# GpSimd makes part of the elementwise sums, and FFN1 of tiles 6 and 7 goes by seven products, in a fused attention and ELU feed-forward kernel

## The chip, the cores and the metric

The kernel runs on one core of a Trainium2 chip. A core has five engines that run side by side: TensorE (PE in the profile, its weight loads PEld), VectorE (DVE), ScalarE (ACT), GpSimd (POOL) and SyncE (SP). The metric is the device time of one execution in microseconds (us). Lower is better.

## The reference

```python
k_all = concat([beacon_k, k], axis=2)          # B=8, H=8, S=576, D=64, 16 beacon keys
scores = q @ k_all^T / sqrt(64)                # causal on the 576 own keys, beacons always seen
a = exp(scores - max); a /= a.sum(-1)
attn = a @ concat([beacon_v, v], axis=2)
x = attn.transpose(0, 2, 1, 3).reshape(4608, 512)
h = x @ w_in                                   # 512 -> 2048  (FFN1)
g = where(h > 0, h, exp(min(h, 0)) - 1)        # ELU
out = g @ w_out                                # 2048 -> 512  (FFN2)
```

Inputs and output are float32. The kernel computes in 16-bit types with float32 accumulation in PSUM.

## The kernel before

Attention goes batch by batch (b = 0 to 7), the feed-forward part by token tiles: tiles 0 and 1 have 256 tokens each, tiles 2 to 9 have 512. The whole program is one list of short step names, `run("""...""")`, written out as a planner left it. Each engine carries out its own instructions in the order of that list and waits by semaphores for what it needs. `S` makes scores on TensorE, `x` their exponential on ScalarE, `m` masks on VectorE. `D.b.d.n` adds the key chunk n+1 of four heads onto a running sum over chunks (L396), so that TensorE makes the softmax sums (`L`, L422) from one chunk instead of five. `n` and `M` turn sums into scale factors and scale the result into `xT`.

FFN1 of a 512-token tile has 16 steps `F.t.i` (L514), each 4 matmuls of 512 columns into one PSUM bank (tag `hps`, two banks). The ELU of a bank is `e` (exp, ScalarE, L524), `u` (relu, L530 on ScalarE or, as `u.v`, L532 on VectorE) and `k` (min of exp-1 and relu, VectorE, L544), or `e`, `r` (L551) and `g` (L556).

FFN2 of every tile but tile 0 alone (0 and 1 together) is a 2x2 block product by seven products instead of eight (`Q`, L618, 112 matmuls of 256 columns a tile). It needs block sums of the activations, `Z.t.1` to `Z.t.4` (L566, 2048 columns each), and of `w_out`, `wt.1` to `wt.4`, made once. `J` drains its products (L628, L633, L635).

FFN1 of the last two tiles (8 and 9) goes by seven products as well: groups `P.t.g.ph` (L706), four groups of 512 features a tile, each 7 x 4 matmuls of 256 columns in place of four `F` steps. They need sums of `w_in`, `H.n.g` (two instructions of 256 columns each) and of the inputs, `X.t.n` (512 columns, L689). `K` drains them: products 0, 2 and 3 are copied out by ScalarE (L716), and products 1, 4 and 5 are added to such a copy by VectorE (L719), so that `E`, `U` and `V` (L728, L735, L737, L745) can make the ELU.

All elementwise sums (`D`, `Z`, `wt`, `H`, `X`) run on VectorE here. GpSimd issues the input loads (`lq`, `lv`, `lk`, `wi`, `wo`) from its queue and does the beacon copies `lp` (L786). SyncE issues the transposing loads `lt` and the output stores.

Of the kernel before, what the change touches and what calls it, by code (L numbers as in the profile page):

```python
# [8 lines left out]
FP32 = mybir.dt.float32  # L9
# [8 lines left out]
def kernel(  # L18
# [12 lines left out]
    P = 128  # L31
# [163 lines left out]
    def bank(tag, dt=FP32, name="bk"):  # L195
        return psum.tile([P, 512 if dt == FP32 else 1024], dt, tag=tag, name=name)
# [184 lines left out]

    presum = {}
# [5 lines left out]
    @step  # L388
    def D_(b, d, n):

        r_ = presum[b, d] = qkp.bitcast(FP16)[:, :, 0:S]
        t = et4(b, d)
        a, e, col = next((a, e, col) for (j, a, e, col) in lays[b] if j == n + 1)
        rows = kc[n + 1]
        o = r_[0:rows, :, a:e]
        nc.vector.tensor_tensor(  # L396
            out=o, in0=t[0:rows, :, a:e] if n == 0 else o, in1=t[0:rows, :, col:col + e - a], op=ALU.add)
# [120 lines left out]
    def flat(y):  # L518
        return y.rearrange("c n w -> c (n w)")
# [45 lines left out]
    def sub(o_, a_, b_, op_=ALU.subtract, eng="v"):  # L565
        (nc.vector if eng == "v" else nc.gpsimd).tensor_tensor(out=o_, in0=a_, in1=b_, op=op_)  # L566

    HP = NPR // 2

    @step  # L570
    def wt(n, h_):
        c = slice(HP * h_, HP * (h_ + 1))
        if n == 1:
            sub(T1[:, c], B12[:, c], B11[:, c])
        elif n == 2:
            sub(T2[:, c], B22[:, c], T1[:, c])
        elif n == 3:
            sub(B12[:, c], B22[:, c], B12[:, c])
        else:
            sub(T4[:, c], B21[:, c], T2[:, c])  # L580
# [92 lines left out]
    def H_(n, g):  # L673
        for kk_ in range(2):
# [4 lines left out]
            sub(o_, x_, y_, f_)  # L679
# [6 lines left out]
    def X_(t, n, eng="v"):  # L686
# [6 lines left out]
          (0, (1, 0), 3, False), (1, 4, (1, 1), False), (0, (1, 1), 4, False)]  # L693
    hx, fm, hb = {}, {}, {}

    @step
    def P_(t, g, ph):
        if (t, g, 0) not in hx:
            for n_ in (0, 1) if g % 2 == 0 else (1, 0):
                hx[t, g, n_] = bank("hps", name="hps").rearrange("c (n w) -> c n w", n=2)  # L700
        n_, a_, b_, first = PF[ph]
        for c in range(2):
# [9 lines left out]
    def K_(t, g, ph, eng="s"):  # L712
        src = flat(hx[t, g, PF[ph][0]])
# [8 lines left out]
    def hsrc(t, g, ph):  # L722
        return flat(hx[t, g, 0]) if ph == 6 else hb[t, g, ph]
# [76 lines left out]
    wm.4 wm.4 warm.4 wm.4 lq.0.0.0.4 lq.0.1.0.4 wm.4 warm.4 ident lq.0.0.4.8 wm.4 T.0.1.0 bt  # L800
    warm.4 lq.0.1.4.8 bk cb.0.3 T.0.0.0 cb.0.1 cb.0.0 ck.0.1.0 S.0.1.0 ck.0.0.0 T.0.1.1 x.0.1.0
    S.0.0.0 x.0.0.0 T.0.0.1 cq.0.1.1 S.0.1.2 cq.0.0.1 T.0.3.0 S.0.0.2 x.0.1.2 T.0.2.0 x.0.0.2
    cq.0.3.0 S.0.0.3 cb.0.2 lq.1.0.0.4 S.0.3.0 T.0.3.1 cq.0.2.0 x.0.0.3 lv.0.0.1 cq.0.3.1
    x.0.3.0 T.0.2.1 S.0.0.1 tri wm.4 x.0.0.1 S.0.3.2 x.0.3.2 S.0.1.3 cq.0.2.1 x.0.1.3 wm.4 wm.4
    S.0.2.0 wm.4 wm.4 x.0.2.0 S.0.3.3 wm.4 x.0.3.3 S.0.2.3 x.0.2.3 wm.4 m.0.3.0 S.0.3.1 cb.1.0
    x.0.3.1 lv.0.2 m.0.1.0 m.0.2.0 m.0.0.0 L.0.A m.0.1.2 n.0.A m.0.0.2 T.1.0.0 wi.2 m.0.3.2
    cq.1.0.0 S.0.2.1 W.0.A.1 x.0.2.1 W.0.A.0 S.0.1.1 x.0.1.1 T.1.1.0 M.0.A.1 S.0.2.2 M.0.A.0
    x.0.2.2 F.0.5 cq.1.1.0 e.0.5 lv.0.3.4 m.0.2.2 wi.1 m.0.0.3 m.0.1.3 S.1.5 S.1.1 x.1.5 m.0.3.3
    F.0.4 x.1.1 lq.1.0.4.8 wi.0 m.0.2.3 L.0.B cb.1.1 e.0.4 W.0.B.1 n.0.B S.1.3 cb.1.3 u.0.4.v
    M.0.B.1 u.0.5.v F.0.2 x.1.3 e.0.2 r.0.2 S.1.4 x.1.4 S.1.0 x.1.0 F.0.3 T.1.3.0 ck.1.3.0  # L810
    W.0.B.0 g.0.2 wi.3 k.0.4 S.1.12 m.1.0.0 k.0.5 M.0.B.0 e.0.3 F.0.1 x.1.12 T.1.2.0 S.1.10
    r.0.3 g.0.3 F.1.0 cq.1.2.0 cb.1.2 e.0.1 u.0.1 x.1.10 k.0.1 F.1.1 e.1.0 S.1.8 lq.2.0.0.4
    u.1.1.v u.1.0 k.1.0 x.1.8 F.0.0 e.1.1 S.1.9 S.1.6 u.0.0.v lq.2.0.4.8 F.0.6 k.1.1 x.1.9
    lp.3.1 e.0.0 T.2.1.0 F.1.3 x.1.6 u.0.6.v e.0.6 cq.2.1.0 S.1.11 cb.2.0 lv.1.0.1 e.1.3 x.1.11
    S.1.7 k.0.0 F.0.7 S.1.2 u.1.3.v F.1.5 x.1.7 x.1.2 T.2.0.0 k.0.6 lv.1.2.3.4 u.0.7.v e.0.7
    m.1.1.1 T.2.2.0 ck.2.0.0 u.1.5.v ck.2.2.0 m.1.1.0 wo.1 e.1.5 m.1.0.1 F.1.6 wo.3 k.0.7 L.1.1
    L.1.0 wo.0 F.1.2 e.1.6 wo.2 k.1.5 lk.3.0 u.1.6.v lk.3.1 F.1.4 cb.2.1 cb.2.2 n.1.1 M.1.1.0
    W.1.0 k.1.6 n.1.0 M.1.0.0 u.1.2 W.1.1 lv.2.2.3.4 u.1.4 M.1.0.1 lk.4.0 e.1.2 lv.3.2.3.4 k.1.3
    S.2.4 e.1.4 x.2.4 F.1.7 M.1.1.1 k.1.4 u.1.7 e.1.7 F.2.13 T.2.3.0 S.2.8 u.2.13 k.1.7 F.2.12
    e.2.13 x.2.8 F.2.9 u.2.12 cq.2.3.0 S.2.3 e.2.12 k.2.13 S.2.1 e.2.9 wt.1.0 k.1.2 x.2.3 F.2.2  # L820
    e.2.2 lv.2.0.1 Z.1.3.B Q.1.0.7 x.2.1 Q.1.7.14 u.2.9.v S.2.2 S.2.0 u.2.2 k.2.12 F.2.6 k.2.9
    Q.1.14.21 x.2.0 x.2.2 F.2.15 cb.2.3 wt.1.1 e.2.6 wt.2.1 u.2.6 u.2.15 Q.1.21.28 e.2.15
    m.2.0.0 S.2.6 S.2.5 wt.2.0 F.2.4 J.1.0 x.2.5 F.2.10 Z.1.1.B Z.1.2.B S.2.11 x.2.6 Q.1.28.35
# [121 lines left out]
```

## Time and profile before

| | before |
|---|---|
| runs | 330.08, 330.23 (median), 334.53 us |
| profiled execution | 329.86 us, of which the span is 328.2 us, clock 1.000 |
| PE busy | 318.5 us (97%) |
| PEld busy | 215.7 us (66%) |
| DVE busy | 296.9 us (90%) |
| ACT busy | 276.4 us (84%) |
| POOL busy | 85.2 us (26%), nearly all of it issuing DMAs |

Busy time is the time in which at least one instruction ran. An instruction's own duration is somewhat longer than its share of busy time, since neighbours on one engine overlap by some 0.08 us. The span runs from the first to the last instruction; 1.7 us of the execution lie around it.

### The profile page before, as it was taken

The page shows a single profiled execution, that of the slowest core. Times are in us where ns is not written, and L with a number is a line of the kernel's source. Part 1 is how long each engine was busy: PE and PEld are TensorE (multiplying, and loading weights), DVE is VectorE, ACT ScalarE, POOL GpSimd, SP SyncE. Part 2 cuts the span into 40 slices and gives each one's busy share as a digit, 9 for nine tenths or more (in the row PEclk, how much of TensorE's full clock was granted, in tenths as well). Part 3 has the DMA queues.
Part 4 walks back from the last instruction along what each step waited for, and adds up shares of the span by engine and source line. Part 5 has one row for each costly group of instructions (what it writes and reads, how often), then busy time and mean ns, then how long its engine had stood idle before and what let it go on. Part 6 is the DMA issues. An engine that isn't in the chain of part 4 may idle for free.

```text
span 328.2 us, 8827 instructions
## 1 busy us (share of the span) xinstructions
PE 318.5 (97%) x3648; PEld 215.7 (66%) x3648; DVE 296.9 (90%) x527; ACT 276.4 (84%) x449; POOL 85.2 (26%) x109
## 2 busy tenths in 40 slices
PE   7879999999999999999999999999999999999995
PEld 4656766566555655566555665566665888888884
DVE  2677998999998999999989989999999999999992
ACT  2979999998889897999999888988699598889930
POOL 8973791742705626004010500000000000000000
PEclk9999999999999999999999999999999999999999
DMA  9999999999999999995922792010110021111113
GB/s 115 169 190 206 172 167 185 151 151 154 174 173 154 136 172 151 188 116 61 160 82 58 77 106 84 12 34 2 66 34 33 2 96 34 34 65 34 35 64 128
DMA packets 130520, 34.65 MB, mean 106 GB/s; under 512 B 112816, under 2 KB 130480, under 8 KB 130480
## 3 DMA queue, kind: packets, MB, share of 16 engines
q0 software_dynamic: 95840, 18.49, 69.1%
q1 hardware_dynamic: 33920, 15.34, 23.8%
q8 instruction: 28, 0.46, 0.6%
q10 hardware_dynamic: 720, 0.26, 0.3%
q14 instruction: 12, 0.10, 0.1%
HBM read 37.22 MB, written 15.34 MB: 160 GB/s over the span
## 4 chain that ended last, share of the span: by engine, by line
PE 72%; DMA 12%; ACT 7%; POOL 4%; DVE 3%; issue 2%; DVEq 0%; POOLq 0%
PE ops L618 27%; PE hps L514 22%; DMA v<-in_v_dram 10%; PE hps L706 8%; PE sc L318 5%; ACT et L333 5%; PE ut L376 5%; PE sx L618 2%; POOL scr L769 1%; POOL v L149 1%; DMA kst<-in_k_dram 1%; ACT e L524 1%; POOL w_out L163 1%; DVE qkp L396 1%; PE lt L422 1%
## 5 line engine op out<-in xcount | busy, mean ns | idle before, releaser
L333 ACT ACTIVATE et<-sc 128x1024 f16<-128x1024 f32 (+2 forms) x114 | 104.2, 968 | 8.1 <-PE sc L318 7.6
L514 PE MATMUL hps<-xT,w_in 128*128 128x512 f16 (+1 forms) x512 | 110.7, 353 | 0.3 <-DVE gt L556 0.3
L618 PEld LDWEIGHTS <-gt 128*128 128x128 f16 x864 | 83.0, 98 | 21.1 <-issue 2.9
L524 ACT ACTIVATE e<-hps 128x512 f32<-128x512 f32 x112 | 66.7, 615 | 9.0 <-PE hps L514 4.1
L514 PEld LDWEIGHTS <-w_in 128*128 128x128 f16 x512 | 46.8, 98 | 39.0 <-issue 5.5
L544 DVE SCALAR_TENSOR_TENSOR gt<-e,r 128x512 f16<-128x512 f32 x103 | 68.6, 683 | 2.2 <-ACT e L524 0.7
L618 PE MATMUL ops<-w_out,gt 128*128 128x256 f16 x416 | 54.7, 273 | 0.0
L618 PE MATMUL ops<-wt,gt 128*128 128x256 f16 x400 | 53.6, 273 | 0.0
L530 ACT ACTIVATE r<-hps 128x512 f16<-128x512 f32 x74 | 45.0, 616 | 4.5 <-PE hps L514 4.3
L149 POOL DMA_DIRECT2D v<-in_v_dram x40 | 36.4, 1016 | 3.5 <-DMA v<-in_v_dram 1.9
L566 DVE TENSOR_TENSOR gt<-gt 128x2048 f16<-128x2048 f16 (+1 forms) x30 | 33.1, 1110 | 0.1
L338 DVE TENSOR_TENSOR et<-et,triu 128x1024 f16<-128x1024 f16 (+4 forms) x66 | 26.6, 447 | 1.8 <-ACT et L333 1.7
L532 DVE TENSOR_SCALAR r<-hps 128x512 f16<-128x512 f32 x29 | 19.9, 685 | 4.0 <-ACT e L524 3.2
L376 PEld LDWEIGHTS <-v 128*32 128x32 f16 (+1 forms) x800 | 17.2, 96 | 9.4 <-issue 1.2
L745 DVE SCALAR_TENSOR_TENSOR gt<-e,r 128x512 f16<-128x512 f32 x32 | 21.5, 683 | 0.5 <-ACT kst L716 0.4
L376 PE MATMUL ut<-et,v 128*32 128x464 f16 (+3 forms) x560 | 21.1, 296 | 0.3 <-DMA v<-in_v_dram 0.3
L396 DVE TENSOR_TENSOR qkp<-qkp,et 128x1344 f16<-128x1344 f16 (+2 forms) x33 | 19.2, 583 | 0.4
L635 DVE TENSOR_TENSOR osb<-ops,sm 128x512 f32<-128x512 f32 x26 | 17.7, 682 | 1.3 <-PE ops L618 1.3
L716 ACT COPY kst<-hps 128x512 f32<-128x512 f32 x24 | 13.9, 589 | 4.8 <-PE hps L706 4.6
L474 DVE TENSOR_TENSOR xT<-ut,rl 128x672 f16<-128x672 f32 (+12 forms) x26 | 16.4, 669 | 0.7 <-PE ut L376 0.4
L618 PE MATMUL ops<-w_out,s 128*128 128x256 f16 x128 | 16.9, 273 | 0.0
L618 PEld LDWEIGHTS <-s 128*128 128x128 f16 x144 | 13.9, 98 | 2.5
(118 smaller groups left out, 415.7 us busy)
## 6 DMA issues: line engine op xcount, KB each, us to landing
out_dram<-osb SPq DMA_DIRECT2D x35, 256.0 KB, 2.2
v<-in_v_dram POOLq DMA_DIRECT2D x24, 128.0 KB, 11.8
scr<-in_q_dram POOLq DMA_DIRECT2D x5, 576.0 KB, 16.2
scr<-in_k_dram POOLq DMA_DIRECT2D x5, 576.0 KB, 18.1
w_in<-in_moe_w_in_dram POOLq DMA_DIRECT2D x8, 256.0 KB, 8.7
w_out<-in_moe_w_out_dram POOLq DMA_DIRECT2D x4, 512.0 KB, 10.5
qst<-in_q_dram POOLq DMA_DIRECT2D x4, 288.0 KB, 9.6
kst<-in_k_dram POOLq DMA_DIRECT2D x4, 288.0 KB, 10.0
```

Source lines behind the costliest of these rows:

```text
L149: nc.gpsimd.dma_start(out=vt[b][r0:r0 + n, j, :, :], in_=v[b, :, ilo[j]:ilo[j] + n, :].rearrange("h s d -> s h d"),)
L333: nc.scalar.activation(out=ets[b, d][:, :, a - EC2 * d:e - EC2 * d], in_=sc[b, g][:, :, a - c0:e - c0], func=AFT.Exp, bias=0.0, scale=SCALE)
L338: nc.vector.tensor_tensor(out=o, in0=o, in1=i, op=ALU.mult)
L376: nc.tensor.matmul(out=t[32 * i:32 * (i + 1), a - qa:e - qa], lhsT=ones[0:kc[j], :] if half is None else v16[0:kc[j], j, h, half:D:2], rhs ...
L396: nc.vector.tensor_tensor(out=o, in0=t[0:rows, :, a:e] if n == 0 else o, in1=t[0:rows, :, col:col + e - a], op=ALU.add)
L514: nc.tensor.matmul(out=h[:, n_, :], lhsT=w_in16[:, cc, P * fc:P * (fc + 1)], rhs=xt[k][:, cc, a - TT * k:e - TT * k], start=(cc == 0), sto ...
L524: nc.scalar.activation(out=eb[t, i], in_=flat(hp[t, i]), func=AFT.Exp, bias=0.0, scale=1.0)
L530: nc.scalar.activation(out=rb[t, i], in_=flat(hp[t, i]), func=AFT.Relu, bias=0.0, scale=1.0)
L544: nc.vector.scalar_tensor_tensor(out=half(t, i), in0=eb[t, i], scalar=1.0, in1=rb[t, i], op0=ALU.subtract, op1=ALU.min)
L566: (nc.vector if eng == "v" else nc.gpsimd).tensor_tensor(out=o_, in0=a_, in1=b_, op=op_)
L618: nc.tensor.matmul(out=half_of(xy[t, n_], qd), lhsT=lw[:, P * qd:P * (qd + 1)], rhs=wt_[:, c, :], start=(first and c == 0 and (qd == 0 or ...
L706: nc.tensor.matmul(out=hx[t, g, n_][:, c, :], lhsT=lw, rhs=rh, start=(first and c == 0 and k_ == 0), stop=(k_ == 1), skip_group_check=True)
```

## The change

Four things change, and the whole order list is written anew (the same set of steps otherwise).

1. `D`, `wt` and `H` get an engine argument, which `Z` and `X` had already. A step with `.p` runs as one `nc.gpsimd.tensor_tensor` (two for `H`). On GpSimd now: 19 of 44 `D`, 15 of 40 `Z` (13 of 2048 and 2 of 1024 columns), 4 of 8 `wt`, 11 of 16 `H`, and 8 of 16 `X`: 68 instructions.
2. Seven more FFN1 groups go by seven products: groups 0 to 2 of tile 6 and 0 to 3 of tile 7. 28 `F` steps with their `e`, `u` and `k` go, 49 `P` steps with `K`, `E`, `U`, `V`, and 8 `X` come.
3. In tiles 8 and 9 product 0 goes into a tile of the scores' PSUM tag `S`, ScalarE copies it into a new `hps` bank, and product 1 accumulates on top of the copy. The addition `K.t.g.1` by VectorE falls away in these eight groups.
4. Some drains move between ScalarE and VectorE: `J.v` 10 to 15, `K.v` 0 to 10 (3 of them are step 3's copies, which stay on ScalarE), `U.v` 4 to 19, `u.v` 29 to 32, the form with `r` and `g` 9 to 14, one `ck` to `cq`.

```diff
+    def sub(o_, a_, b_, op_=ALU.subtract, eng="v"):
+        (nc.vector if eng == "v" else nc.gpsimd).tensor_tensor(out=o_, in0=a_, in1=b_, op=op_)
...
-    def D_(b, d, n):
+    def D_(b, d, n, eng="v"):
...
-        nc.vector.tensor_tensor(
-            out=o, in0=t[0:rows, :, a:e] if n == 0 else o, in1=t[0:rows, :, col:col + e - a], op=ALU.add)
+        sub(o, t[0:rows, :, a:e] if n == 0 else o, t[0:rows, :, col:col + e - a], ALU.add, eng)
...
-    def wt(n, h_):
+    def wt(n, h_, eng="v"):
...
-    def H_(n, g):
+    def H_(n, g, eng="v"):
...
-            sub(o_, x_, y_, f_)
+            sub(o_, x_, y_, f_, eng)
...
+    PA = [0, 1, 0, 2, 0, 2, 0]
...
     def P_(t, g, ph):
-        if (t, g, 0) not in hx:
+        seed = t >= 8
+        if seed and ph == 0:
+            hx[t, g, 0] = psum.tile([P, 2, 512], FP32, tag="S", name="sa")[:, 0, :].rearrange("c (n w) -> c n w", n=2)
+        if seed and ph == 3:
+            hx[t, g, 2] = bank("hps", name="hps").rearrange("c (n w) -> c n w", n=2)
+        if not seed and (t, g, 0) not in hx:
...
+        if seed:
+            n_ = PA[ph]
+            first = first and ph != 1
...
     def K_(t, g, ph, eng="s"):
-        src = flat(hx[t, g, PF[ph][0]])
+        if t >= 8 and ph == 0:
+            hx[t, g, 1] = bank("hps", name="hps").rearrange("c (n w) -> c n w", n=2)
+            nc.scalar.copy(out=flat(hx[t, g, 1]), in_=flat(hx[t, g, 0]))
+            return
+        src = flat(hx[t, g, (PA[ph] if t >= 8 else PF[ph][0])])
...
     def hsrc(t, g, ph):
+        if t >= 8 and ph == 1:
+            return flat(hx[t, g, 1])
         return flat(hx[t, g, 0]) if ph == 6 else hb[t, g, ph]
```

In the new list GpSimd's sums stand between its DMA issues, for example (GpSimd's own order) `wt.1.0`, `lk.3.1`, `lk.4.0`, part of `lv.2`, `wt.1.1`, `H.1.0`. Some neighbours on VectorE read what GpSimd writes: `Z.5.2` and `Z.6.2` follow `Z.5.1.p` and `Z.6.1.p`, `D.4.0.2` follows `D.4.0.0.p` and `D.4.0.1.p`.

252 lines of the change are left out of this document (130 added, 122 removed).

## The prediction

> **What bounds the kernel now.** First the busy times, then the long middle stretch alone.
>
> ```profile
> PE 318.5 (97%) x3648; PEld 215.7 (66%) x3648; DVE 296.9 (90%) x527; ACT 276.4 (84%) x449; POOL 85.2 (26%) x109
> ```
>
> ```profile
> 0.00:66.00 66.00, 61.13 (x1050) 41.23 (x1050) 50.89 (x111) 57.03 (x82) 44.75 (x63) 1.00 1.52 169
> 66.00:320.00 254.00, 252.83 (x2564) 170.63 (x2559) 244.07 (x413) 219.02 (x367) 40.45 (x46) 1.00 0.81 88
> 320.00:328.20 8.20, 4.58 (x42) 3.84 (x40) 1.97 (x4) 0.37 (x1) 0.00 (x0) 1.00 0.38 128
> ```
>
> The lower rows are the view by stretches: PE, PEld, DVE, ACT and POOL busy in each. In the 254 us from 66 to 320 TensorE idles 1.2 us, so it sets the end. VectorE idles 9.9 us: it is second by a hair. Whatever lengthens VectorE's queue by more than some 10 us in this stretch makes VectorE the bound; that is the number to carry on. ScalarE has 35 us to spare, GpSimd 213.
>
> **VectorE's work by ports.** An instruction with two SBUF inputs will matter apart from one that reads PSUM. The groups by line and shape (last but one column: busy us, mean ns):
>
> ```profile
> L544 DVE SCALAR_TENSOR_TENSOR gt<-e,r 128x512 f16<-128x512 f32 x103 | 68.6, 683 | 2.2 <-ACT e L524 0.7 <-PE ops L618 0.7 <-ACT r L530 0.4
> L566 DVE TENSOR_TENSOR gt<-gt 128x2048 f16<-128x2048 f16 x24 | 29.2, 1217 | 0.1
> ...
> L396 DVE TENSOR_TENSOR qkp<-et 128x1856 f16<-128x1856 f16 x11 | 12.3, 1115 | 0.1
> ...
> L396 DVE TENSOR_TENSOR qkp<-qkp,et 128x1344 f16<-128x1344 f16 x11 | 9.3, 848 | 0.1
> ...
> L396 DVE TENSOR_TENSOR qkp<-qkp,et 128x832 f16<-128x832 f16 x11 | 6.4, 583 | 0.1
> ...
> L396 DVE TENSOR_TENSOR qkp<-qkp,et 80x320 f16<-80x320 f16 x11 | 3.5, 316 | 0.2
> ...
> L566 DVE TENSOR_TENSOR wt<-w_out,wt 128x1024 f16<-128x1024 f16 x4 | 2.7, 684 | 0.0
> ...
> L566 DVE TENSOR_TENSOR w_in<-w_in 128x256 f16<-128x256 f16 x8 | 1.9, 284 | 0.0
> ```
>
> Busy time from 66 to 320 us of the six lines whose inputs are both in SBUF, in the order L544, L338, L566, L396, L745, L689:
>
> ```profile
> 66.00:320.00 254.00, 57.10 (x86) 1.00 0.81 88
> ...
> 66.00:320.00 254.00, 18.42 (x35) 1.00 0.81 88
> ...
> 66.00:320.00 254.00, 52.55 (x75) 1.00 0.81 88
> ...
> 66.00:320.00 254.00, 31.50 (x44) 1.00 0.81 88
> ...
> 66.00:320.00 254.00, 21.52 (x32) 1.00 0.81 88
> ...
> 66.00:320.00 254.00, 3.35 (x8) 1.00 0.81 88
> ```
>
> They sum to 184.4 us. The other 244.1 - 184.4 = 59.7 us have at most one SBUF input.
>
> **Taken off VectorE.** `Z`: 13 x 1.217 + 2 x 0.684 = 17.2 us. `D` by its shapes (6, 5, 4 and 4 of them): 6 x 1.115 + 5 x 0.848 + 4 x 0.583 + 4 x 0.316 = 14.5. `wt`: 4 x 0.684 = 2.7. `H`: 11 x 2 x 0.284 = 6.2. The new `X` replace nothing: 8 of 16 stay on VectorE as before. Sum 40.6 us, all with two SBUF inputs.
>
> **Added by the seven products and the moved drains.** The rows:
>
> ```profile
> L532 DVE TENSOR_SCALAR r<-hps 128x512 f16<-128x512 f32 x29 | 19.9, 685 | 4.0 <-ACT e L524 3.2 <-PE hps L514 0.3
> ...
> L719 DVE TENSOR_TENSOR kst<-hps,kst 128x512 f32<-128x512 f32 x12 | 8.2, 685 | 0.5 <-PE hps L706 0.2 <-ACT kst L716 0.2
> ...
> L737 DVE TENSOR_SCALAR r<-kst 128x512 f16<-128x512 f32 x3 | 1.3, 421 | 0.0
> ```
>
> ```profile
> L530 ACT ACTIVATE r<-hps 128x512 f16<-128x512 f32 x74 | 45.0, 616 | 4.5 <-PE hps L514 4.3
> L716 ACT COPY kst<-hps 128x512 f32<-128x512 f32 x24 | 13.9, 589 | 4.8 <-PE hps L706 4.6 <-issue 0.2
> ```
>
> VectorE: the `k` and `V` together go from 135 to 130 (-5 x 0.683 = -3.4, two SBUF inputs). The adds of `K` go from 24 to 37: 21 in tiles 6 and 7, 16 in tiles 8 and 9, where the copy into PSUM has taken one of three. That is 13 x 0.685 = 8.9. 15 more `U.v` at 0.421 are 6.3. 20 more drains from PSUM (3 `u.v`, 7 copies of `K`, 5 `J.v`, 5 `g`) at 0.685 are 13.7; 5 `r` and one `cq` are some 4 (estimate from the 0.421 and twice the 0.685). So two-input work becomes 184.4 - 40.6 - 3.4 = 140, one-input work 59.7 + 33 = 93, in all 233 against 244: **VectorE itself is 11 us lighter**.
>
> ScalarE: 36 `u` go and 13 `U` come (-23 x 0.616 = -14), 14 more copies (24 to 38) add 8, five `J` and one `ck` less take 4: 10 us lighter. It stays hidden. The copy into PSUM costs ScalarE the 0.589 that the copy to SBUF cost; product 1 now waits for it, but the list puts a product of another group or phase and mostly a block of `Q` between, 0.4 to 1.2 us of TensorE work. Uncovered, eight such copies would cost 8 x 0.589 = 4.7 us.
>
> TensorE: starts give the rate, since ends are modelled.
>
> ```profile
> 243.82 1.73 PE hps L514 x8
> ```
>
> ```profile
> 262.53 0.60 PE L706 MATMUL hps<-qst,w_in 128*128 128x256 f16 x4
> 262.96 0.93 PE L618 MATMUL ops<-wt,gt 128*128 128x256 f16 x7
> ```
>
> Eight matmuls of 512 columns take 1.73 us in the chain that ended last, 0.216 each. Four of 256 columns take 262.96 - 262.53 = 0.43, 0.108 each. A group by `F` is 16 x 0.216 = 3.46 us, by seven products 28 x 0.108 = 3.02. Seven groups save 7 x 0.44 = **3.0 us on the engine that bounds**. Nothing else on TensorE changes in size. If this were all, the profiled 329.86 would become 326.9.
>
> **What GpSimd's sums cost.** No two-input sum on GpSimd is in the trace. Its one-input sums and their neighbours on VectorE are:
>
> ```profile
> L238 POOL TENSOR_SCALAR_AFFINE_SELECT triu<-triu 128x256 f16<-128x256 f16 x1 | 0.4, 402 | 0.0
> ...
> L238 POOL TENSOR_SCALAR_AFFINE_SELECT triu<-triu 128x128 f16<-128x128 f16 x1 | 0.3, 287 | 0.1
> ```
>
> 128 more columns cost 115 ns: 0.90 ns a column and 172 ns fixed. The 68 sums have 13 x 2048 + 2 x 1024 (`Z`) + 6 x 1856 + 5 x 1344 + 4 x 832 + 4 x 320 (`D`) + 4 x 1024 + 22 x 256 + 8 x 512 = 64,960 columns. Low end, as if a second input were free: 58 + 68 x 0.172 = 70 us. High end, as if it cost a pass of its own: 117 + 12 = 128 us. I take 128, since each sum reads twice what these rows read. A `Z` of 2048 columns is then 3.9 us in place of 1.2.
>
> The Trainium skill ("GPSIMD Engine Reference", section 3.1) gives 4497 ns for a float32 sum of 2048 columns, its two inputs sharing one read port; by that price the sums would take some 149 us (estimate from that page) and the forecast below would be 21 us higher. No run shown here has such a sum.
>
> **Do the two engines run side by side?** The decisive rows, GpSimd's first, then VectorE's, from the timeline (start, duration):
>
> ```profile
> 143.66 0.21 POOL L786 COPY qst<-bkT 128x32 bf16<-128x32 bf16 x1 [12.65 <-PE sc L318]
> 170.26 0.93 POOL L786 COPY kst<-bkT 128x32 bf16<-128x32 bf16 x1 [13.69 <-PE sc L318]
> 104.68 4.12 POOL L149 DMA_DIRECT2D v<-in_v_dram  x4
> ```
>
> ```profile
> 143.62 0.68 DVE L635 TENSOR_TENSOR osb<-ops,sm 128x512 f32<-128x512 f32 x1
> 169.90 1.22 DVE L566 TENSOR_TENSOR s<-gt 128x2048 f16<-128x2048 f16 x1
> 105.60 1.02 DVE L551 TENSOR_SCALAR r<-e 128x512 f16<-128x512 f32 x1 [1.20 <-ACT e L524]
> ```
>
> The view of line L551 (min, median, max in ns):
>
> ```profile
> L551 DVE TENSOR_SCALAR r<-e x9: 412/427/1020, 30.1 to 168.2; 128x512 f16<-128x512 f32 x9
> ```
>
> The same small copy takes 0.21 us beside `J`'s add, which reads PSUM and one SBUF input, but 0.93 under a `Z`, and ends at 171.19 just behind the `Z` at 171.12. GpSimd stood still while VectorE read two SBUF inputs. In the other direction an SBUF-to-SBUF `r` took 1.02 us, against a median of 0.427, while GpSimd wrote DMA descriptors: VectorE stands still too. The trace doesn't show VectorE's two-input work behind a long GpSimd read, since GpSimd has none yet.
>
> The Trainium skill ("SBUF — State Buffer", section "Who interferes with whom") says that VectorE instructions with two SBUF inputs and GpSimd instructions that read SBUF share a read interface, that whichever starts first holds it for its whole length, and that the other blocks. The 0.93 us copy agrees.
>
> **The sum.** Behind a GpSimd sum VectorE can go on only with one-input work; its queue is in order, so the first `k`, `V`, mask or `D` stops it, and the drains behind that stop TensorE. Of the 128 us at most 93 can be covered (all one-input work). At least the run of one-input instructions up to the next two-input one is: about 147 of the former and 200 of the latter (93 / 0.63, 140 / 0.70, estimates), so 0.74 such instructions, 0.46 us, behind each of 68 sums, 31 us. Half way is 62. The stall is then 128 - 62 = 66 us (bounds 35 and 97; at the low price 0 and 39). VectorE's stretch becomes 233 + 66 = 299 us in place of 254, and the 3 us of TensorE vanish behind it. **329.86 + 45 = 375 us**; the profiled execution is within 0.4 us of the median of 330.23, so this is taken as 375. Bounds: 329.86 - 254 + 233 + 97 = 406 at the top. At the low price with 31 us covered the stall is 39 and the time 348; with 62 covered it is 8, which the 21 us that VectorE then has spare swallow, and that is rival A. The likeliest case's own range is 345 to 410.
>
> **Rivals.** *TensorE still bounds (A).* GpSimd's sums are near the low price and stand beside one-input work: nothing is stalled and the time is 326.9, no change. For it speaks GpSimd's idle 213 us; against it the two reads a sum.
>
> *Faster (B).* No exclusion of long sums: VectorE is 11 us and ScalarE 10 us lighter, so TensorE's small waits go as well. It idles 66 - 61.1 = 4.9 us before 66 us and 3.6 after 320, and the reordered start may win half of the first: 326.9 - 1.2 - 2.5 = 323. Against it stands the 0.93 us copy.
>
> *Slower by late sums alone (C).* Without exclusion a `Z` by GpSimd is 3.9 - 1.2 = 2.7 us later, and 21 VectorE instructions wait in the new list for a GpSimd result, `Z.5.2` and `D.4.0.2` among them. Behind a waiting `Z.t.2` stand `V` and `K`, and for these wait ScalarE's `E` and TensorE's next product. If half of them show 1.5 us: 326.9 + 16 = 343. It decides where GpSimd's price a column is over twice VectorE's 0.6 (1.217 us by 2048).
>
> GpSimd's queue also carries `lv` and `lk`; a sum ahead of them delays a load by up to 4 us. `wt.1.0` waits for `w_out` and stands ahead of `lk.3.1`, `lk.4` and `lv.2`. The list keeps these loads a batch ahead of the `W` and `S` that use them, which is what hides them, so I cost this at nothing; without that cover each would cost up to 4 us.
>
> **Chances.** Exclusion as summed 0.62, C 0.10, A 0.11, B 0.17. Faster by over 2% (under 323.6; 2% is about what a measurement of this kernel can tell from no change) takes B: 0.17. Within 2% A: 0.11. Slower 0.72. The range goes from 322, which leaves out half of B, to 412, which leaves out the dearer prices.
>
> **What the profile after would show.** Right: VectorE instructions with two SBUF inputs (L546, L759, L338) that last or wait several times their 0.68 us, always beside a GpSimd sum; GpSimd's sum of 2048 columns near 4 us; TensorE with idle time put down to VectorE from 70 us on; `P` and `Q` still at 0.108 us a matmul. Wrong: `k` and `V` at 0.68 us beside running sums (B), sums near 2 us (A), or VectorE's idle time put down to GpSimd rather than its instructions stretched (C).

## The result, and the profile after

| | before | after |
|---|---|---|
| median of the runs | 331.27 us (330.08 to 334.53) | 434.83 us (433.62 to 437.16) |
| profiled execution, of it the span | 329.86, 328.2 us | 433.71, 432.0 us |
| TensorE busy, idle in the span | 318.5, 9.7 us | 350.6, 81.4 us |
| VectorE busy, idle in the span | 296.9, 31.3 us | 381.4, 50.6 us |
| mean granted clock of TensorE | 1.000 | 0.912 |

The granted clock is the share of full speed that the profile records for TensorE. The time is 1.311 times that of before (95% interval 1.299 to 1.323). A median here is of all executions of a kernel, while a ratio compares the executions in the faster of two states alone, which moves it by some 1% at most. The forecast was 375 us: the direction is right, and the loss is 103.6 us instead of 45.

The page of the changed kernel, its busy times and the granted clock in 40 slices:

```profile
PE 350.6 (81%) x3732; PEld 236.7 (55%) x3732; DVE 381.4 (88%) x516; ACT 272.3 (63%) x434; POOL 234.0 (54%) x177
...
PEclk9999996989989996999898959888897998997699
```

The view by stretches (PE, PEld, DVE, ACT, POOL busy, then the granted clock), the middle one:

```profile
66.00:424.00 358.00, 287.82 (x2677) 193.72 (x2677) 325.56 (x406) 221.65 (x362) 186.93 (x113) 0.90 0.53 63
```

The stretch is 104 us longer. VectorE has 81.5 us more busy time in it with seven instructions fewer, and still idles 32.4 us, where it idled 9.9. TensorE, which had 1.2 us idle here, has 70.2, and its clock has gone from 1.00 to 0.90.

VectorE's groups by line and shape (busy us, mean ns of one, idle before):

```profile
L546 DVE SCALAR_TENSOR_TENSOR gt<-e,r 128x512 f16<-128x512 f32 x70 | 73.5, 1065 | 3.6 <-ACT r L532 1.9 <-PE ops L617 0.9 <-ACT e L526 0.7
L759 DVE SCALAR_TENSOR_TENSOR gt<-e,r 128x512 f16<-128x512 f32 x60 | 66.1, 1121 | 3.6 <-PE ops L617 1.8 <-ACT e L742 1.3 <-ACT r L749 0.2
L338 DVE TENSOR_TENSOR et<-et,triu 128x1024 f16<-128x1024 f16 x28 | 30.5, 1090 | 1.0 <-ACT et L333 1.0
...
L534 DVE TENSOR_SCALAR r<-hps 128x512 f16<-128x512 f32 x32 | 21.6, 681 | 3.6 <-ACT e L526 1.8 <-PE hps L516 1.8
L634 DVE TENSOR_TENSOR osb<-ops,sm 128x512 f32<-128x512 f32 x26 | 17.7, 680 | 3.4 <-PE sx L617 1.7 <-issue 1.6
```

The first three read two SBUF tiles. The first of them was 683 ns before and is now 1065 in the mean. The last two take an input from PSUM and last what they did before, 680 ns. GpSimd's groups of sums:

```profile
L383 POOL TENSOR_TENSOR gt<-gt 128x2048 f16<-128x2048 f16 x9 | 38.8, 4316 | 44.6 <-PE ops L617 18.0 <-DVE gt L546 14.6 <-DVE s L383 5.7
...
L383 POOL TENSOR_TENSOR qkp<-et 128x1856 f16<-128x1856 f16 x6 | 22.6, 3766 | 42.5 <-ACT et L333 14.9 <-DVE gt L546 12.3 <-PE lt L376 7.6
...
L383 POOL TENSOR_TENSOR s<-gt 128x2048 f16<-128x2048 f16 x4 | 16.6, 4150 | 4.0 <-DVE gt L759 2.7 <-PE hps L714 0.7 <-DVE gt L546 0.6
```

One place in the timeline shows the whole loss in small (start, us). GpSimd, then VectorE, then TensorE:

```profile
242.72 1.36 POOL L383 TENSOR_TENSOR w_in<-w_in 128x256 f16<-128x256 f16 x2
244.02 1.30 POOL L383 TENSOR_TENSOR hi<-lo,w_in 128x256 f16<-128x256 f16 x2
245.28 4.04 POOL L383 TENSOR_TENSOR s<-gt 128x2048 f16<-128x2048 f16 x1
249.40 4.39 POOL L383 TENSOR_TENSOR gt<-gt 128x2048 f16<-128x2048 f16 x1
```

```profile
243.41 10.56 DVE L338 TENSOR_TENSOR et<-et,triu 128x1024 f16<-128x1024 f16 x2
253.89 0.68 DVE L731 TENSOR_TENSOR qst<-hps,kst 128x512 f32<-128x512 f32 x1
```

```profile
227.48 1.70 PE L617 MATMUL ops<-wt,gt 128*128 128x256 f16 x7
...
233.94 0.93 PE L617 MATMUL ops<-wt,gt 128*128 128x256 f16 x7
...
254.62 1.01 PE L714 MATMUL hps<-qst,w_in 128*128 128x256 f16 x4 [8.16 <-DVE qst L731]
...
256.50 1.91 PE L617 MATMUL ops<-wt,gt 128*128 128x256 f16 x8
```

Two masks that take 0.68 and 0.31 us in the kernel without sums on GpSimd need 10.56 us here. The first alone lasts 6.47 us (243.41 to 249.88 in the trace): GpSimd ran three sums of 256 columns and one of 2048 to their ends before it. The second is held by the next sum. `K`'s add stands behind them in VectorE's queue, and TensorE waits 8.16 us for it. Then comes the second part, which the forecast did not have: behind the pause TensorE's products go at half speed. Seven of 256 columns took 1.70 us at 227.48, behind another pause, and 0.93 at 233.94; eight took 1.91 at 256.50.

### The profile page after: what moved, and what is told of

The parts are those of the page before. It is cut to its first block, busy times and chain, and to the rows that moved or that the text cites. A ratio compares the mean times of both kernels' runs of the same rounds, so it can differ in the third digit from the quotient of the medians.

```text
span 432.0 us, 9071 instructions
## 1 busy us (share of the span) xinstructions
PE 350.6 (81%) x3732; PEld 236.7 (55%) x3732; DVE 381.4 (88%) x516; ACT 272.3 (63%) x434; POOL 234.0 (54%) x177
## 5 line engine op out<-in xcount | busy, mean ns | idle before, releaser
L516 PE MATMUL hps<-xT,w_in 128*128 128x512 f16 (+1 forms) x400 | 89.8, 362 | 18.7 <-ACT e L526 11.3
L546 DVE SCALAR_TENSOR_TENSOR gt<-e,r 128x512 f16<-128x512 f32 x70 | 73.5, 1065 | 3.6 <-ACT r L532 1.9
L526 ACT ACTIVATE e<-hps 128x512 f32<-128x512 f32 x84 | 50.2, 608 | 38.3 <-PE hps L516 17.2
L759 DVE SCALAR_TENSOR_TENSOR gt<-e,r 128x512 f16<-128x512 f32 x60 | 66.1, 1121 | 3.6 <-PE ops L617 1.8
L516 PEld LDWEIGHTS <-w_in 128*128 128x128 f16 x400 | 37.0, 100 | 51.5 <-issue 30.4
L383 POOL TENSOR_TENSOR gt<-gt 128x2048 f16<-128x2048 f16 (+1 forms) x10 | 41.0, 4096 | 44.7 <-PE ops L617 18.0
L338 DVE TENSOR_TENSOR et<-et,triu 128x1024 f16<-128x1024 f16 (+5 forms) x66 | 45.8, 731 | 1.1 <-ACT et L333 1.0
L383 POOL TENSOR_TENSOR qkp<-et 128x1856 f16<-128x1856 f16 x6 | 22.6, 3766 | 42.5 <-ACT et L333 14.9
L714 PEld LDWEIGHTS <-w_in 128*128 128x128 f16 x240 | 25.1, 107 | 33.5 <-issue 23.9
L383 POOL TENSOR_TENSOR qkp<-qkp,et 128x1344 f16<-128x1344 f16 (+2 forms) x13 | 27.1, 2086 | 24.7 <-DVE qkp L383 21.9
L532 ACT ACTIVATE r<-hps 128x512 f16<-128x512 f32 x38 | 22.8, 611 | 9.5 <-PE hps L516 4.9
L383 POOL TENSOR_TENSOR s<-gt 128x2048 f16<-128x2048 f16 (+1 forms) x5 | 18.7, 3744 | 13.9 <-PE ops L617 9.9
## 6 DMA issues: line engine op xcount, KB each, us to landing
w_out<-in_moe_w_out_dram POOLq DMA_DIRECT2D x4, 512.0 KB, 10.2
```

The costliest lines, as they stand in the source:

```text
L338: nc.vector.tensor_tensor(out=o, in0=o, in1=i, op=ALU.mult)
L516: nc.tensor.matmul(out=h[:, n_, :], lhsT=w_in16[:, cc, P * fc:P * (fc + 1)], rhs=xt[k][:, cc, a - TT * k:e - TT * k], start=(cc == 0), sto ...
L526: nc.scalar.activation(out=eb[t, i], in_=flat(hp[t, i]), func=AFT.Exp, bias=0.0, scale=1.0)
L532: nc.scalar.activation(out=rb[t, i], in_=flat(hp[t, i]), func=AFT.Relu, bias=0.0, scale=1.0)
L546: nc.vector.scalar_tensor_tensor(out=half(t, i), in0=eb[t, i], scalar=1.0, in1=rb[t, i], op0=ALU.subtract, op1=ALU.min)
L714: nc.tensor.matmul(out=hx[t, g, n_][:, c, :], lhsT=lw, rhs=rh, start=(first and c == 0 and k_ == 0), stop=(k_ == 1), skip_group_check=True)
```

## The experiments

Each kernel is an edit of before or after; medians stand beside the kernel before on the same chip (331.1 to 331.3 us, in the last four runs 330.8).

**Is it exclusion, and of what?** One kernel measures the pairs alone, stretch by stretch: 24 VectorE instructions beside four GpSimd sums of 2048 columns, or eight fills.

```diff
+    stretch(pool_sum, 4, None, 0)     # GpSimd's sums alone
+    stretch(None, 0, two, 24)         # VectorE, two SBUF inputs, alone
+    stretch(pool_sum, 4, two, 24)     # both
+    stretch(pool_sum, 4, one, 24)     # VectorE with one input in PSUM
+    stretch(pool_set, 8, two, 24)     # GpSimd only writes
+    stretch(pool_sum, 4, conv, 24)    # VectorE, one SBUF input, SBUF out
```

> The disputed cost alone; nothing of the reference is computed. Five stretches: 24 VectorE instructions of 512 columns with two SBUF inputs alone (some 16 us); the same beside four GpSimd sums of 2048 columns (some 16 us alone); 24 VectorE adds with one input in PSUM beside four sums; 24 of the first kind beside eight GpSimd memsets of 2048 columns, which read nothing; 24 SBUF-to-SBUF tensor_scalar beside four sums. Exclusion theory: the second stretch lasts as long as both alone, 30 to 33 us, with single VectorE instructions lasting 4 us or more; the third and fourth last as long as the longer engine, 16 to 18 us, and VectorE's instructions keep 0.68. The fifth tells whether a one-input instruction within SBUF is held as well (30 us) or not (17). Rival (GpSimd is merely slow, its results late): every stretch lasts 16 to 18 us and no VectorE instruction is longer than alone.

The timeline, GpSimd and then VectorE:

```profile
9.55 16.41 POOL L49 TENSOR_TENSOR go<-ga,gb 128x2048 f16<-128x2048 f16 x4 [0.28 <-DVE ga L64]
44.03 17.40 POOL L49 TENSOR_TENSOR go<-ga,gb 128x2048 f16<-128x2048 f16 x4 [18.07 <-DVE ga L64]
```

```profile
26.40 17.40 DVE L55 SCALAR_TENSOR_TENSOR vo<-e,r 128x512 f16<-128x512 f32 x24
...
44.12 32.39 DVE L55 SCALAR_TENSOR_TENSOR vo<-e,r 128x512 f16<-128x512 f32 x24
...
76.71 17.36 DVE L58 TENSOR_TENSOR fo<-pt,f 128x512 f32<-128x512 f32 x24
...
96.07 17.40 DVE L55 SCALAR_TENSOR_TENSOR vo<-e,r 128x512 f16<-128x512 f32 x24
...
113.79 25.96 DVE L61 TENSOR_SCALAR vo<-e 128x512 f16<-128x512 f32 x24
```

The 24 two-input instructions take 17.40 us alone, 32.39 beside four sums, 17.40 beside fills; the adds from PSUM take 17.36 beside the sums. So GpSimd's reading excludes VectorE's second SBUF input, and its filling doesn't. The last row was not expected: the conversion from SBUF to SBUF, with one input, is held as well (25.96 us for 24; the same form took 0.427 us at the median in the kernel before, so 10.2 for 24). The Trainium skill ("SBUF — State Buffer", section "Who interferes with whom") names `tensor_scalar` among the operations that can take the shared pair of ports in a 2-port mode and then contend with GpSimd; this row agrees with it.

**How much of the 104 us is GpSimd's reading?** Two kernels keep the order of the changed kernel. In the first GpSimd is as busy, but only writes:

```diff
+        if eng != "v":
+            nc.gpsimd.tensor_tensor(out=o_[:, :, 0:2], in0=a_[:, :, 0:2], in1=b_[:, :, 0:2], op=op_)
+            for _ in range(2):
+                nc.gpsimd.memset(o_, 1.0 if eng == "d" else 0.001)
+            return
```

> The changed kernel with its order as it is, but each GpSimd sum is replaced by a sum of two columns a block (so that it waits for the same data) and two memsets of its whole output, which take about as long as the sum and read nothing; the sums' values are left out. Exclusion theory: VectorE's two-input instructions are back at 0.68 us, VectorE is busy some 287 us, and the time falls to 325 to 345. Rival (late sums): results come as late as before, so the time stays above 410. Rival (the other parts of the change cost the time): stays above 410 too.

In the second every `.p` is taken off the order list, so that VectorE makes all sums.

> The changed kernel and order with every sum back on VectorE. Exclusion theory and late-sum theory alike: GpSimd's part is the whole loss; VectorE is busy 381 - 94 + 41 + 3 = 331 us, bounds the kernel, and the time is 340 to 365. Rival (seven products, copy in PSUM, moved drains or the new order cost the time): above 390.

```profile
PE 322.6 (95%) x3732; PEld 226.2 (66%) x3732; DVE 294.9 (86%) x516; ACT 270.0 (79%) x434; POOL 238.7 (70%) x313
```

```profile
PE 323.1 (91%) x3732; PEld 224.4 (63%) x3732; DVE 326.9 (92%) x584; ACT 271.8 (76%) x434; POOL 87.1 (24%) x109
```

Fills only: 339.91 us, 1.027 (1.021 to 1.033) of before. No sums: 358.37, 1.084 (1.078 to 1.089). The first is the best control there is: the same order and the same 516 VectorE instructions, GpSimd busy 238.7 us against 234.0. Its span is 341.0. So of the 103.8 us that the span has grown, **91.0 go with GpSimd's reading** and 12.8 with all the rest. By engine, reading costs VectorE 381.4 - 294.9 = 86.5 us of held time, and TensorE 28.0 us of busy time and 63.0 of idle. The second gives the size of the sums: 234.0 - 87.1 = 147 us of GpSimd.

The control isn't wholly free of holds. Its conversions from SBUF to SBUF (min, median, max in ns) reach 2.03 us beside a fill:

```profile
L756 DVE TENSOR_SCALAR r<-kst x10: 414/534/1994, 215.1 to 316.4; 128x512 f16<-128x512 f32 x10
L756 DVE TENSOR_SCALAR r<-qst x8: 422/464/2033, 218.3 to 322.3; 128x512 f16<-128x512 f32 x8
```

Held time can be counted for each VectorE instruction, as its duration less the median of the same shape in the kernel with no sums on GpSimd. That gives 94.5 us in the changed kernel and 8.2 in the control, nearly all of the latter in such conversions. Without its held time VectorE has 286.9 and 286.7 us of work in the two, against 296.9 before.

**How does a held VectorE become lost time?** To have it in a quiet place, the kernel before was given only seven sums on GpSimd: `Z.t.4` of tiles 2 to 8.

```diff
-    Z.2.4.B ... Z.8.4.B
+    Z.2.4.B.p ... Z.8.4.B.p
```

> The kernel before and its order, with one sum alone moved: the fourth block sum of tiles 2 to 8, seven of 2048 columns, on GpSimd. No VectorE instruction reads these sums and TensorE needs them a dozen blocks of Q later. Exclusion theory: VectorE gains 7 x 1.2 = 8.5 us and is held 7 x (4.1 - 0.5) = 25 us, with 10 us of idle time to cover: 6 to 16 us slower, 336 to 347. Rival (late sums): nothing waits, 327 to 332.

358.82 us, 1.080 (1.072 to 1.087): 27.6 us for seven sums, 3.9 us a sum, which is about what one lasts; the expectation was 6 to 16. Six kernels take this apart. The control, in which GpSimd fills instead of sums as above:

> The kernel before, in which GpSimd is given the fourth gate sum of tiles 2 to 8 as in the run before, but makes only two columns of each as a sum and fills the rest twice with a constant, so that it is busy about as long (7 x 3.7 us) and reads nothing (those seven operands are wrong). The exclusion theory, with a held VectorE starving TensorE: GpSimd's writes hold nobody, VectorE is 8.5 us lighter, so 327 to 334 us. The rival, that the 27 us came because TensorE waited for a sum that is ready 3 us later: 350 to 362 us, as with the real sums.

331.53 us, 1.001 (0.997 to 1.005). A sum that is ready late costs nothing here; all 27 us are the reading.

The same seven sums in eight pieces each, first with a filler behind each piece (`nc.gpsimd.memset(spare, 0.0)`, 384 columns), then without:

```diff
+            for i_ in range(8):
+                nc.gpsimd.tensor_tensor(out=o_[:, i_:i_ + 1], in0=a_[:, i_:i_ + 1], in1=b_[:, i_:i_ + 1], op=op_)
```

> The kernel before, GpSimd makes the same seven sums, each in eight pieces of 256 columns with a filler of 384 columns behind each piece (writes only), so that the same reading (some 30 us in all) comes in holds of 0.7 us instead of 4.2 us. Theory that the length of a hold decides (TensorE has work of 2 to 3 us in its banks, so a short hold costs it nothing and its clock stays): 333 to 342 us, and no half-clock windows after the sums. The rival, that held time adds up whatever its length: 350 to 362 us.

> As the run with eight pieces of 256 columns, without the filler between the pieces: the same reading, back to back. Theory that GpSimd keeps VectorE out across instructions that follow each other at once: one hold of 4 us or more each time, 352 to 365 us as with whole sums. The rival, that VectorE gets in between any two instructions, so that the pieces alone did it: 335 to 343 us.

339.07 us (1.024, 1.017 to 1.030) with fillers and 337.95 (1.018, 1.010 to 1.025) without. Pieces cost far less, and the fillers don't matter. GpSimd does not keep VectorE out across a row of instructions in these two kernels (it does in another, below). The timeline without fillers, GpSimd and then VectorE:

```profile
145.57 7.34 POOL L568 TENSOR_TENSOR gt<-gt 128x256 f16<-128x256 f16 x8 [10.82 <-DVE gt L570]
```

```profile
145.87 0.91 DVE L544 SCALAR_TENSOR_TENSOR gt<-e,r 128x512 f16<-128x512 f32 x1 [0.15 <-ACT e L524]
...
149.01 1.62 DVE L396 TENSOR_TENSOR qkp<-et 128x1856 f16<-128x1856 f16 x1
```

VectorE goes on between the pieces and loses some tenths of a microsecond at a time; GpSimd's eight pieces take 7.34 us in place of 4.25. So the two engines alternate here, and what VectorE's next instruction pays is the length of one GpSimd instruction. Counted as above against the kernel before, VectorE is held 24.7 us with the seven whole sums and 13.5 with pieces: there is less held time, and a microsecond of it costs about half (6.7 us of loss for 13.5, against 27.6 for 24.7).

Is the loss GpSimd's doing, or would any 4-us absence of VectorE do it? In two kernels GpSimd makes no sum, and VectorE gets 70 sums of 384 columns into a tile that nobody reads: ten in a row behind each `Z.t.4`, or one at a time behind the next VectorE steps.

```diff
+    def hold(w_):
+        nc.vector.tensor_tensor(out=spare[:, 0:w_], in0=spare[:, 0:w_], in1=spare[:, 0:w_], op=ALU.add)
...
-    Z.2.4.B
+    Z.2.4.B hold.384 hold.384 hold.384
...
```

> The kernel before with no sum on GpSimd. Behind each of the seven fourth gate sums VectorE makes ten more sums of 384 columns into a tile that nobody reads, some 2.7 us, so that it is away from its drains for about 4 us with no GpSimd in it; 19 us of VectorE work more. Theory that a 4-us absence of VectorE is what costs (and not something that GpSimd does to TensorE): 345 to 362 us with half-clock windows behind each. The rival, that GpSimd's reading itself slows TensorE or ScalarE: 331 to 340 us.

> The same 70 extra VectorE sums of 384 columns as in the run before, but one at a time behind the next VectorE steps instead of ten in a row. If the length of an absence decides: 333 to 343 us, at least 8 us under the run with ten in a row. If only VectorE's total work decides, the two are equal within 3 us.

The timeline of the ten in a row, VectorE and then TensorE:

```profile
157.22 1.21 DVE L568 TENSOR_TENSOR gt<-gt 128x2048 f16<-128x2048 f16 x1
158.35 3.89 DVE L572 TENSOR_TENSOR spare<-spare 128x384 f16<-128x384 f16 x10
162.16 0.68 DVE L534 TENSOR_SCALAR r<-hps 128x512 f16<-128x512 f32 x1
```

```profile
158.69 1.03 PE L516 MATMUL hps<-xT,w_in 128*128 128x512 f16 x4
162.89 1.02 PE L516 MATMUL hps<-xT,w_in 128*128 128x512 f16 x4 [3.18 <-DVE r L534]
```

The pages of the two, in a row and spread:

```profile
PE 329.7 (91%) x3648; PEld 219.6 (61%) x3648; DVE 322.1 (89%) x598; ACT 276.9 (77%) x449; POOL 84.8 (23%) x109
...
PEclk9989999999999899998999999999998999899899
```

```profile
PE 322.5 (94%) x3648; PEld 215.7 (63%) x3648; DVE 314.9 (92%) x598; ACT 277.3 (81%) x449; POOL 84.4 (25%) x109
...
PEclk9999999999999999999999999999999999999999
```

363.72 us in a row (1.098, 1.092 to 1.105), 348.21 spread (1.053, 1.045 to 1.060). The same 598 VectorE instructions cost 15.5 us more where they stand together. VectorE is away for 5 us (157.22 to 162.16), and TensorE, 2.5 us into it, has nothing left to do and stands for 3.18. In a row it has seven such pauses of 2.9 to 3.7 us, one for each `Z.t.4`, five of them with a window at half clock behind; spread it has no pause over 2 us and no dip before the last microseconds. Part of the 15.5 us is VectorE's own: ten sums in a row on one tile keep it busy 7.2 us longer (322.1 against 314.9). GpSimd makes no sum in either, so an absence of VectorE is enough to make the pauses and the half clock, whoever keeps it away. The spread kernel was slower than expected (333 to 343): 18 us of busy time added to VectorE (314.9 against 296.9) cost 17 even so.

The pauses by themselves, TensorE alone, with bursts of 140 products and VectorE work of known length between:

```diff
+    for us10 in (4, 10, 15, 20, 25, 30, 35, 40):
+        gap(us10 * 96)     # VectorE reads the result, works, writes the next operand
+        burst(140)         # 140 matmuls of 256 columns
```

> Computes nothing of the reference: TensorE alone, bursts of 140 products of 256 columns, and between two bursts a pause that VectorE's work sets, some 0.7, 1.3, 1.8, 2.3, 2.8, 3.3, 3.8 and 4.3 us, three times over. Theory that a pause of TensorE of about 3.4 us or more costs it its clock: behind the three or four longest pauses the first products take twice as long (0.22 us apiece instead of 0.11) for 3 us or more, behind the shorter ones none. The rival, that the half clock in the changed kernel has another cause than the pauses (the current drawn, or GpSimd's work): no burst is slow behind any pause.

The timeline, and the view by stretches right behind the two pauses (products in brackets, the granted clock before the last two columns):

```profile
71.64 3.54 PE L48 MATMUL pt<-x,wts 128*128 128x256 f16 x31 [2.40 <-DVE x L54]
...
153.00 9.24 PE L48 MATMUL pt<-x,wts 128*128 128x256 f16 x71 [4.40 <-DVE x L54]
```

```profile
71.70:75.10 3.40, 3.40 (x32) 3.05 (x32) 0.00 (x0) 0.00 (x0) 1.00 0.00 0
...
153.00:156.40 3.40, 3.40 (x19) 2.48 (x19) 0.00 (x0) 0.00 (x0) 0.59 0.00 0
156.40:159.80 3.40, 3.40 (x34) 3.04 (x32) 0.00 (x0) 0.00 (x0) 1.00 0.00 0
```

After a pause of 2.40 us 32 products start in 3.4 us, after one of 4.40 only 19. Over the three rounds, counted product by product in the trace, no burst was slow behind pauses of 0.8 to 2.4 us (12 of 12), two of three behind 2.9, and all nine behind 3.4 to 4.4. The slow time is a window of 3.41 us at half clock, twice a double one. That is close to what the Trainium skill says ("TensorE: Matmul & The Clock Gate", Part 1): half clock after about one idle window of some 3.4 us, full clock again after about as long a busy one. Here 2.9 us was at times enough. In the kernels themselves shorter pauses were, too: with the seven whole sums the granted clock was 0.52 in the 3.4 us behind a pause of 2.28 us, and in the changed kernel with its sums in pieces without fillers (next part) 40 products of `ut`, which take 1.51 us elsewhere, took 2.61 behind one of 2.11:

```profile
162.65 0.38 PE L428 MATMUL lt<-qkp,ones 128*32 128x464 f16 x4 [2.11 <-DVE qkp L387]
...
162.99 2.61 PE L376 MATMUL ut<-et,v 128*32 128x464 f16 x40
```

**Does this mend the changed kernel?** Its sums in pieces along one dimension, most of 256 columns, with and without fillers:

```diff
+            for i_ in range(o_.shape[1]):
+                nc.gpsimd.tensor_tensor(out=o_[:, i_:i_ + 1], in0=a_[:, i_:i_ + 1], in1=b_[:, i_:i_ + 1], op=op_)
```

> The changed kernel, every GpSimd sum in pieces of up to 512 columns with a filler of 384 columns (writes only) behind each: the same reading, in short holds; GpSimd is busy longer, some 300 us, and its sums are ready later. Theory that the long holds and the half clock behind them make most of the loss: 365 to 395 us, granted clock 0.98 or more, VectorE held some 50 us instead of 94. The rival, that the total of the reading or lateness of the sums makes it: 430 us or more.

> The changed kernel with every GpSimd sum in pieces along one dimension (most of 256 columns, the block sums of 208 to 464), with no filler between them. In the run with fillers GpSimd was busy 380 us of 443, so its sums came late; without fillers some 320. Theory that the length of a hold makes the loss in the changed kernel as it did for the seven sums alone: 375 to 410 us. The rival, that here the sum of all reading and the late sums decide, whatever the length: 425 us or more.

```profile
PE 347.9 (78%) x3732; PEld 234.1 (53%) x3732; DVE 362.7 (82%) x516; ACT 273.5 (62%) x434; POOL 380.2 (86%) x637
```

```profile
PE 333.9 (83%) x3732; PEld 229.3 (57%) x3732; DVE 368.6 (91%) x516; ACT 272.6 (68%) x434; POOL 305.1 (76%) x373
```

With fillers 442.93 us (1.324, 1.311 to 1.338): a miss, nothing is gained. GpSimd is then busy 380.2 us and its sums come late: VectorE's `Z` instructions wait 19.7 us for them, 10.4 of it at one place. Without fillers 410.13 us (1.233, 1.223 to 1.244), at the upper edge of what was expected: 25 of the 95 us between 434.8 and 339.9 come back. VectorE is still held 368.6 - 294.9 = 73.7 us of the 86.5. Why short pieces do so much less here than for the seven sums alone is in part to be seen in the timeline without fillers, GpSimd, VectorE and TensorE:

```profile
240.60 5.05 POOL L385 TENSOR_TENSOR s<-gt 128x256 f16<-128x256 f16 x8
245.62 5.02 POOL L385 TENSOR_TENSOR gt<-gt 128x256 f16<-128x256 f16 x8
```

```profile
241.74 11.59 DVE L763 SCALAR_TENSOR_TENSOR gt<-e,r 128x512 f16<-128x512 f32 x2
```

```profile
254.32 1.25 PE L621 MATMUL ops<-w_out,gt 128*128 128x256 f16 x5 [8.47 <-DVE osb L636]
```

The first of the two `V` lasts 10.98 us of the 11.59: GpSimd finishes 19 pieces in a row before it, and TensorE stands for 8.47. A `Z` at 298.32 lasts 11.88 us behind 16 pieces in the same way, and TensorE stands for 11.46. So cutting a sum does not by itself make the holds short: here the two engines alternate at most places, and at these GpSimd keeps VectorE out for many instructions. What decides between the two is not known, and how much of the remaining loss is long holds and how much the sum of the short ones was not separated.

Is it one kind of sum, or their number? All sums back on VectorE but the gate sums (15 `Z`), or but the block sums (19 `D`):

> The changed kernel, of whose GpSimd sums only the 15 gate sums (Z, some 61 us of reading) stay on GpSimd; the block, chunk and weight sums are VectorE's again. If each microsecond of reading costs the same, on the line from no sum on GpSimd (358 us, no reading) to all (435 us, 150 us of reading): 386 to 392 us. If the loss comes from sums that queue behind each other on GpSimd and are late (all kinds share it): under 375 us.

> The changed kernel, of whose GpSimd sums only the 19 block sums (D, some 48 us of reading) stay on GpSimd. By the same line from 358 to 435 us: 380 to 386 us. If the loss is from late sums in a shared queue: under 370 us.

```profile
PE 340.3 (85%) x3732; PEld 233.1 (58%) x3732; DVE 355.7 (89%) x569; ACT 272.0 (68%) x434; POOL 148.3 (37%) x124
```

```profile
PE 331.0 (87%) x3732; PEld 228.6 (60%) x3732; DVE 345.6 (91%) x565; ACT 271.5 (71%) x434; POOL 135.9 (36%) x128
```

Only `Z`: 404.53 us, more than either theory said. Only `D`: 383.10 us, on the line. Against the 358.4 without sums on GpSimd, `Z` costs 46 us for 148.3 - 87.1 = 61 us of reading and `D` 25 us for 49. Together 71 of the 76 us that all cost: the losses nearly add up, so a shared queue of late sums is not the reason.

**The rest of the change.** Only the copy into PSUM (part 3), in the order of before:

```diff
-    P.8.0.0 ... P.8.0.1 K.8.0.0 ... P.8.0.2 ... K.8.0.1
+    P.8.0.0 ... K.8.0.0 ... P.8.0.2 P.8.0.1 ...
```

> The kernel before with only the last part of the change: in the last two tiles product 0 is copied into the next PSUM tile and product 1 is added to it there; no group more, no sum on GpSimd. TensorE does the same work, VectorE eight adds of 0.68 us fewer in the last 60 us: 327 to 332 us, no difference that can be told or one below 1%. The rival, that the wait of product 1 for the copy costs TensorE at each group: 334 to 342 us.

331.97 us, 1.003 (1.000 to 1.006): no difference that can be told. Last, the changed kernel with no sum on GpSimd and ScalarE in place of VectorE in `U`, `J` and `K`:

```diff
-    J.1.0.v ... K.6.0.0.v ... U.6.0.5.v
+    J.1.0 ... K.6.0.0 ... U.6.0.5
```

> The changed kernel with no sum on GpSimd, and all 44 drains and half products of the steps U, J and K that VectorE makes given to ScalarE, so that VectorE has some 27 us less to do and ScalarE some 27 us more. Theory that the run without GpSimd sums was 27 us over the kernel before because VectorE had become the engine that the order waits for: 333 to 345 us. The rival, that the seven more groups or their order cost this whoever drains them: 352 us or more.

```profile
PE 324.4 (91%) x3732; PEld 224.6 (63%) x3732; DVE 308.5 (86%) x542; ACT 290.4 (81%) x476; POOL 86.5 (24%) x109
```

359.82 us, 1.087 (1.082 to 1.092), as with VectorE's drains (358.37). VectorE is 18 us lighter and TensorE idles 33.3 us against 33.2. My reading of the 27 us that the order costs without GpSimd, VectorE's load, falls. What it is stays open: the list was written for another sharing of the work, and TensorE's idle time lies in many waits of 1 to 2 us for VectorE and ScalarE in turn.

## Why the prediction was wrong in size

- **Exclusion** was the mechanism, as summed: two SBUF inputs last longer beside a GpSimd sum, a PSUM input doesn't, and the fill-only control is 95 us faster.
- **Price of the sums**: nearly right. 128 us were taken; by the shortest of each shape in the changed kernel the sums themselves are some 135 (2048 columns: 4.04 in place of 3.9). The 147 of GpSimd's busy time hold some 15 us more, in which a sum itself stood behind VectorE. The figure named beside it from the Trainium skill ("GPSIMD Engine Reference", section 3.1), 149 us, comes near the 147, but by chance: it was worked out from a float32 sum and stands 14 us above the sums' own price.
- **VectorE 11 us lighter**: right. Without its held time VectorE has 286.9 us of work against 296.9 before, 10 less.
- **Covered part**: mis-sized. 62 us were taken, half way between two bounds, for no stronger reason. In the trace VectorE did 38.9 us of work beside the sums in instructions that weren't held (not over 0.25 us longer than their median), near the lower bound of 31. One reason is that the conversions from SBUF to SBUF, counted as cover, are held too: one of line L751 takes 3.94 us in place of 0.43. So 94.5 us are held where 66 were forecast, inside the bounds of 35 and 97.
- **The step that failed: VectorE's stretch is its busy time, 233 + 66 = 299 us in place of 254.** That lets the 21 us by which VectorE had become lighter than the old stretch swallow the first 21 of the holds, and takes it that VectorE has no idle time left beyond the 9.9 us of before. The stretch is 325.6 us busy and 32.4 idle, 358.0. For the whole span the forecast comes to 286 us of work, 66 held and 21 idle; measured are 287, 94.5 and 50.6. So of the 59 us that the forecast is short, 28.5 are longer holds (23 from the cover, the rest from the price) and 29 the idle time.
- **What the idle time is.** With fills VectorE idles 46.1 us as well (341.0 - 294.9). The holds, 86 us more than with fills, on balance used none of that up, and the span grew by 91.0. (How much of the 50.6 was there already and how much came anew behind holds was not taken apart.) The seven sums alone say the same: VectorE idled 46.8 us in that run (360.2 - 313.4), and 24.7 us of holds cost 27.6. The likely reason, not tested apart, is that idle time elsewhere in the queue does not help at the place of a hold, where TensorE runs dry some 2.5 to 3 us in (3 at 243.41, 2.5 in the run with ten sums in a row). On TensorE's side, fills against sums: 63.0 us more idle, and 28.0 us more busy for the same 3732 matmuls. The clock explains most of the latter: a mean of 0.912 over 432.0 us means 0.088 x 2 x 432 = 76 us at half speed, with fills (0.985 over 341.0) 10 us; 28 us in 66 is 0.42 a microsecond, where 0.5 would be lost if TensorE always had work. The forecast's mark that `P` and `Q` stay at 0.108 us a matmul is refuted by the rows at 227.48 and 256.50, which last twice as long.
- **Rivals.** A and B fall with exclusion. C, late sums without exclusion at 343 us, is near the fill-only kernel's 339.9, but that kernel's 9 us hold the rest of the change and the held conversions as well, and were not taken apart. One late sum is to be seen there: TensorE stands 4.26 us at 89.4 for a `wt`.
- **Steps costed at nothing.** The copy into PSUM was right. GpSimd's loads behind its sums were not tried alone; the fill-only kernel, with GpSimd as busy ahead of them, bounds them with all else at 9 us. The 3.0 us that TensorE was to save did not show: TensorE is busy 322.6 us with fills against 318.5.

No version tried beats the kernel before; the nearest are the copy into PSUM alone (1.003) and the seven fills (1.001, part of the result left out).

## What to carry to other kernels

Before work goes to an idle engine, ask which port it reads through and who is in front of it in a queue: here sums that kept GpSimd busy for 147 us made VectorE stand still for 86 us longer than fills did. When an engine that feeds the bound is kept away, price the single absence against the buffers between them (here two banks, some 2.5 us of work), and add what the starved engine's clock loses afterwards; short absences spread out cost about half of what the same work cost in a row (17 us against 32), and idle time that an engine has elsewhere does not pay for them. A sum over one engine's busy time is a lower bound of the span once two in-order engines wait for each other in turn.

## What the runs showed of the hardware that was not expected

- VectorE's SBUF-to-SBUF conversion with a single input is held by GpSimd's reads (25.96 us for 24 beside four sums, about 10 alone) and by its fills (up to 2.03 us for one of 0.42).
- GpSimd and VectorE can alternate instruction by instruction when both have one ready: eight pieces of 256 columns took 7.34 us, with VectorE at work between, against 4.25 for the whole sum. But they need not: one VectorE instruction was held 10.98 us while 19 pieces ran.
- A TensorE pause of 2.9 us or more can cost a window of 3.41 us at half clock. With bursts of matmuls alone, 2.4 us or less never did, behind 12 pauses; in two of the kernels pauses of 2.11 and 2.28 us did.
